# Local and global attention, then eight experts: the first four units in another order, V of batch 1 in later slots, stores of stage two in the middle of the next group

## The chip, the cores and the metric

The kernel runs on one core of a Trainium2 chip. The core's engines each work through a list of their own: PE (TensorE) does matmuls and transposes into PSUM, DVE (VectorE), ACT (ScalarE) and POOL (GpSimd) do the element work, SP only issues DMAs; ACT and POOL issue some as well. Semaphores order the lists against each other. The metric is the device time of one execution in microseconds, as the median over runs; lower is better.

## What is computed

Attention over 8 batches and 8 heads: 512 local positions that see the 32 global keys and a band of 32 positions to each side, and 32 global positions that see everything. Its output, as 4352 rows of 512, goes through a mixture of 8 experts whose weights per row come from a softmax that is normalised over rows and columns eight times.

```python
k_all = np.concatenate([k_g, k_l], axis=2); v_all = np.concatenate([v_g, v_l], axis=2)
out_g = np.matmul(sm(scale * np.matmul(q_g, k_all.transpose(0, 1, 3, 2))), v_all)
s_ll = np.where(np.abs(pos[:, None] - pos[None, :]) <= 32,
                scale * np.matmul(q_l, k_l.transpose(0, 1, 3, 2)), -1e9)
s_lg = scale * np.matmul(q_l, k_g.transpose(0, 1, 3, 2))
out_l = np.matmul(sm(np.concatenate([s_lg, s_ll], axis=-1)), v_all)
x = np.concatenate([out_g, out_l], axis=2)      # rows of H*D = 512
P = np.exp(x @ w_gate - max)
for _ in range(8):                               # rows, then columns
    P /= P.sum(1, keepdims=True) + 1e-09
    P /= P.sum(0, keepdims=True) + 1e-09
    P *= N / E
out = sum(P[:, e:e+1] * (np.maximum(x @ w1[e], 0.0) @ w2[e]) for e in range(E))
```

## The kernel before

The order of the instructions is written out by hand (`manual_schedule`): each engine runs its part in the order of the Python code, and waits where data or a buffer is not ready. DMAs of SP, ACT and POOL stand in those engines' lists too.

**Stage one** is attention. A *unit* `n` is a pair of heads of a batch (4 units to a batch, 32 in all). Its steps:

- `st_A(n)`, L260: PE transposes q and k; DVE copies the keys to `kTe`, ACT spreads the queries to `qbd`.
- `st_B(n, part)`, L281, and for batch 0 `st_B0`, L308: scores of eight windows of 128 keys and the 32 global keys, in three parts. In `st_B0` the mask is added by a matmul (L325), DVE takes the extreme of each row (L330) and ACT the exponential with its row sum (L334). Two parts use PSUM buffers of `ps_sc`, the third one of `ps_mm`.
- `st_N`, L337: DVE divides by the row sums (L341, L342) and POOL does the global keys' part into `Pl` (L346).
- `st_D1`, L349, and `st_D2`, L357: PE transposes the weights; DVE copies the first (`pw`, L355), ACT the second (`pg`, L363).
- `st_E`, L365: PE multiplies with V (`vab`, `vgz`), and ACT writes the result to `xT` (L379).

`select_v`, L145, lays V of a batch out in rows, in two forms (`va`, `vb`), by matmuls with a selection matrix; each of its slots `j` is four matmuls of 512 columns (L150) and a copy from PSUM (L152) by DVE or ACT. It reads `vsr`, which POOL casts (`cast_vrow`, L139) from what `load_vrow` has loaded. Batch 0 needs four slots of each form, batch 1 four of the first and one of the second; two DMAs on ACT (L604, L605) make the rest of the second form of batch 1. Later batches are loaded in other ways.

The loop at L538 runs over the first four units (`s` = 0 to 3), without any expert work. The loop at L585 runs over the other slots; from its first slot on, matmuls of experts 0 and 1 (`f1`, `f2`, L457 and L471) fill PE between the steps. PSUM is full: two buffers each in `ps_mm`, `ps_sc` and `ps_tr`, and one, of two banks, in `ps_po`.

SP's list holds, in this stretch and in order: the vz loads of batch 0, q and k of batch 1, first half, eight loads of `k_g` (L190), V of batch 1, q and k of batch 1, second half, eight loads of `q_g`, four loads of `vgz` of batch 1 (L159, which read what POOL's DMA at L155 wrote), and q and k of batch 2 (L118). A DMA that uses a semaphore again waits until the one before it on that semaphore has landed.

**Between the stages** the gate's probabilities are normalised while the rest of experts 0 and 1 runs.

**Stage two** runs over groups `m` (512 rows; the last, `m` = 8, has 256) and experts 2 to 7, one pair to an iteration of the loop at L908. An iteration multiplies the rows with `w1` of the next pair (`l1`, L741) and does seven products for its own (`product`, L769), which at a group's last expert are added to `o` (L791). SP loads `w1` two pairs ahead (`load_w1`, two buffers), the scaling rows `pb` three ahead, and at expert `e == 4` the start values of the next group (`load_y`, two buffers of `o`). After a group's last pair, `store(m)` writes `o` to the output.

Of the kernel before, what the change touches and what calls it, by code (L numbers as in the profile page):

```python
# [10 lines left out]
FP32 = mybir.dt.float32  # L11
# [12 lines left out]
def kernel(  # L24
# [13 lines left out]
    nc = tc.nc  # L38

    B, H, Sl, Dh = q_l.shape  # L40
    Sg = q_g.shape[2]
    D, E = moe_w_gate.shape
# [45 lines left out]
    with tc.tile_pool(name="att_c", bufs=1) as att_c, \  # L88
# [50 lines left out]
        def cast_vrow(b):  # L139
            f = vraw.pop(b)  # L140
            for g in range(2):
                h = slice(4 * g, 4 * g + 4)
                nc.gpsimd.tensor_copy(out=vsr[:, :, h, :], in_=f[:, h].rearrange("p h s d -> p s h d"))

        def select_v(b, t, js, both=True):  # L145
            for j in js:
                c0 = P * j + HB * t
                pv = ps_mm.tile([P, D], FP32, tag="mm", name="pv")
                for so in range(NJ):
                    nc.tensor.matmul(pv, zsel[:, so, c0 : c0 + P], vsr[:, so], start=(so == 0), stop=(so == NJ - 1))  # L150
                cp = nc.vector.tensor_copy if both and j % 2 == 0 else nc.scalar.copy
                cp(out=vab[b % 2][t][:, j], in_=pv.rearrange("p (h d) -> p h d", h=H))  # L152

        def load_vg(b):
# [2 lines left out]
        def load_vz(b):  # L157
            for i in range(4):
                nc.sync.dma_start(out=vgz[b % 2][W * i : W * (i + 1), i], in_=vg16[b])  # L159
# [28 lines left out]
        def load_g(src, f):  # L188
            for b in range(B):
                nc.sync.dma_start(out=f[GP * b : GP * (b + 1)], in_=src[b].rearrange("h (p s) d -> p h (s d)", s=NJ))  # L190
# [23 lines left out]
        def init_vgz(t, eng):  # L214
            eng.memset(t, 0.0)
# [121 lines left out]
        def st_N(n, i0, i1):  # L337
            d = st[n]
            if i0 == 0:
                d["rs"] = att_wk.tile([P, NHB], FP32, tag="rs", name="rs")  # L340
            nc.vector.reciprocal(out=d["rs"][:, i0:i1], in_=d["sm"][:, i0:i1])  # L341
            nc.vector.tensor_tensor(out=d["Pu"][:, i0:i1, 0:KW], in0=d["Pu"][:, i0:i1, 0:KW],  # L342
                                    in1=d["rs"][:, i0:i1].unsqueeze(2).to_broadcast([P, i1 - i0, KW]), op=ALU.mult)
            if i1 == NHB:
                d["Pl"] = att_wk.tile([P, NHB, Sg], FP16, tag="Pl", name="Pl")
                nc.gpsimd.tensor_tensor(out=d["Pl"], in0=d["Pu"][:, :, KW:SW],  # L346
                                        in1=d["rs"].unsqueeze(2).to_broadcast([P, NHB, Sg]), op=ALU.mult)
# [188 lines left out]
        cast_first(0, 1, nc.scalar.copy)  # L536
        cast_first(1, 1, nc.vector.tensor_copy)
        for s in range(HP):  # L538
            if s >= 1:
                st_D1(s - 1)  # L540
                st_D2(s - 1)
            for part in range(3):
                st_B0(s, part)
            if s == 0:
                cast_vrow(0)
                cast_qk(0, 1, gq)
                load_qk(1, 0, (nc.sync, nc.sync))
                load_g(k_g, kgf)
                load_w1e(0)
                nc.vector.memset(qbd[1], 0.0)  # L550
            elif s == 1:
                load_vrow(1)
                load_qk(1, 1, (nc.sync, nc.sync))
                load_g(q_g, qgf)
                load_vg(1)
                init_vgz(vgz[1], nc.gpsimd)
            elif s == 2:
                load_w2e(0)
                nc.gpsimd.dma_start(out=wg_sb, in_=moe_w_gate.rearrange("(dko dki) e -> dki dko e", dki=P))
                cast_qk(1, 0, gq)  # L560
                gk0 = cast_g(kgf, 0)
                load_vz(1)
            for t in (kTe[s + 2],) if s < 3 else kTe[5:7]:
                nc.vector.memset(t[:, 0:W], 0.0)
                nc.vector.memset(t[:, W + Sl :], 0.0)
            st_A(s + 1)
            st_N(s, 0, 6)
            st_N(s, 6, NHB)
            if s == 1:
                select_v(0, 1, range(NJ))  # L570
            if s >= 1:
                st_E(s - 1)
            if s == 0:
                select_v(0, 0, range(NJ))
            if s == 3:
                transpose_g(gk0, 0, kgT)
                for t in qgbd:
                    nc.vector.memset(t, 0.0)
                cast_vrow(1)
                load_w1e(1)  # L580
                nc.vector.memset(mask[:, :, KW:SW], 0.0)
                nc.scalar.mul(mask[:, :, 0:KW], m16, -HUGE * 8.0)
        gat = {s: s - 5 for s in range(5, 9)}
        gat.update({2 * j + 1: j for j in range(4, NU // 2)})
        for s in range(HP, NU + 1):  # L585
            slot = s
            b, hp = divmod(s, HP)
            g1 = s in gat
            g23 = s - 1 in gat
            if g1:  # L590
                gn = divmod(gat[s], 2)
            if g23:
                gp = divmod(gat[s - 1], 2)
            if s == HP:
                st_D1(s - 1)
                st_D2(s - 1)
                select_v(1, 0, range(2), False)
                st_E(s - 1)
                select_v(1, 0, range(2, NJ), False)
                st_B(s, 0)  # L600
                select_v(1, 1, (NJ - 1,), False)
                slot = s + 1
                va, vb = vab[1]
                nc.scalar.dma_start(out=vb[0:HB, 0 : NJ - 1], in_=va[HB:P, 0 : NJ - 1])  # L604
                nc.scalar.dma_start(out=vb[HB:P, 0 : NJ - 1], in_=va[0:HB, 1:NJ])  # L605
                cast_qk(1, 1, gq)
                load_w2e(1)
            else:
                st_D1(s - 1)
                if g23:  # L610
                    st_GN(*gp)
            if g1 and s > HP + 1:
                st_G0(*gn)
            f1("a")
            f1("a")
            if HP < s < NU:
                st_B(s, 0)
            if s > HP:
                st_D2(s - 1)
            if g23:  # L620
                st_G2(*gp)
            if s < NU:
                st_B(s, 1)
            f2("a")
            if s + 1 < NU:
                st_A(s + 1)
            f1("v")
            if s < NU:
                st_B(s, 2)
                st_N(s, 0, 6)  # L630
            if s > HP:
                st_E(s - 1)
            if s == HP + 1:
                for t, (src, g, dst) in gcast:
                    transpose_g(t, g, dst)
                st_G0(*gn)
            if g23:
                st_G3(*gp)
            f2("a")
            if s < NU:  # L640
                st_N(s, 6, NHB)
            if s == HP:
                gcast = [(cast_g(x[0], x[1]), x) for x in ((kgf, 1, kgT), (qgf, 0, qgT), (qgf, 1, qgT))]
            if s > 2 * HP:
                f1("v")
            if s >= 5 and (s - 5) % HP == 0:
                logits(NJ * ((s - 5) // HP), NJ)
            if g1:
                st_G1(*gn)
            if s < NU and b + 1 < B:  # L650
                if hp == 0:
                    load_qk(b + 1, 0, (nc.sync, nc.sync))
                    load_qk(b + 1, 1, (nc.sync, nc.sync))
                elif hp == 1:
                    cast_qk(b + 1, 0, gq)
                    if b >= 2:
                        load_w1d(b)
                elif hp == 2:
                    vq = load_v(b + 1)
                    run(vq[:3])  # L660
                    cast_qk(b + 1, 1, gq)
                else:
                    run(vq[3:])
            if s == NU - 3:
                load_w1d(E - 1)
# [242 lines left out]
    for i, (m, e) in enumerate(egs):  # L908
        load_w1(i + 2)
        load_pb(i + 3)  # L910
        if e == 4:
            load_y(m + 1)
        if i == NEG_ - 1:
            last_pair(i)
            break
        sums(i)
        if e == 2 and i > 0:
            init_o(m)
        scale_x(i + 2)
        if m == 0 and e + 2 < E:  # L920
            prep_w2c(e + 2)
        for fm in range(3):
            l1(i + 1, fm, ps_rot, "r")
        for q, fm in ((3, 3), (4, 4), (5, 5), (2, 6), (1, 7), (6, None), (7, None)):
            if i == 0 and q == 2:
                init_o(m)
            product(i, q)
            if fm is not None:
                l1(i + 1, fm, ps_rot, "r")
        if e == E - 1:  # L930
            store(m)
    ctx1.__exit__(None, None, None)


# [28 lines left out]
```

## Time and profile before

| | |
|---|---|
| median of 3 runs | 1077.34 us (1076.32 to 1077.87) |
| the profiled execution | 1076.56 us |
| its span, first to last instruction | 1074.8 us |
| PE, DVE, ACT, POOL busy in the span | 1037.4, 687.3, 553.7, 137.2 us |
| mean granted PE clock | 0.988 |

Busy us by stretches of the span:

| stretch | PE | DVE | ACT | granted clock | DMA share |
|---|---|---|---|---|---|
| 0 to 10 us (loads, first casts) | 7.20 | 8.72 | 3.90 | 1.00 | 0.87 |
| 330 to 400 (normalising) | 68.40 | 41.71 | 35.45 | 1.00 | 0.94 |
| 1035 to 1075 (last group) | 31.58 | 20.07 | 12.85 | 0.96 | 0.39 |

The profile gives for each instruction its engine, its line in the kernel, its start and its length, and for idle time what ended it. PE's matmuls overlap one another, so the time from one start to the next is what a matmul costs, and the length shown is longer. A DMA that has been issued lands some us later.

### The profile page before, as it was taken

Reading aid. Unit: us, or ns where it says so; the run is one execution under the profiler, and the core shown is the slowest. Engines: PE = TensorE matmul, PEld = TensorE weight load, DVE = VectorE, ACT = ScalarE, POOL = GpSimd, SP = SyncE. Lnnn points to the kernel's source line nnn. Section 1 sums busy time; section 2 is a strip of 40 time slices with the busy share of each in tenths; the row PEclk is TensorE's granted clock in tenths of the full one; section 3 lists DMA queues with packets and bytes.
Section 4 is the critical chain, followed back from the end, with each engine's and each line's share of the span. In section 5 each row is a group of like instructions: output and inputs, shape, how many; then the busy total and the mean of one; then the engine's idle time right before and its main releaser. Section 6 shows DMA issues by size and latency. Waiting matters only on the chain.

```text
span 1074.8 us, 20827 instructions
## 1 busy us (share of the span) xinstructions
PE 1037.4 (97%) x8444; PEld 665.1 (62%) x8444; DVE 687.3 (64%) x1438; ACT 553.7 (52%) x1345; POOL 137.2 (13%) x224
## 2 busy tenths in 40 slices
PE   7778999999999999999999999999999999999987
PEld 3445555555555456666666666666666666666676
DVE  7566776766675757766576576575484484485475
ACT  5768787787876445334343343343343343343332
POOL 7243413413314300000000000000000000000000
PEclk9789999999999999999999999999999999999999
DMA  9837677677745975423524524425334234234242
GB/s 280 159 104 161 100 181 153 145 176 140 167 104 100 237 229 198 176 98 138 182 93 167 188 82 162 177 99 175 138 138 176 100 138 176 101 144 150 102 159 82
DMA packets 95799, 160.57 MB, mean 149 GB/s; under 512 B 32716, under 2 KB 68696, under 8 KB 84696
## 3 DMA queue, kind: packets, MB, share of 16 engines
q1 hardware_dynamic: 45208, 119.98, 32.4%
q0 software_dynamic: 46736, 20.20, 15.3%
q10 hardware_dynamic: 3760, 19.07, 4.5%
q8 instruction: 66, 1.08, 0.4%
q14 instruction: 29, 0.24, 0.1%
HBM read 149.24 MB, written 33.40 MB: 170 GB/s over the span
## 4 chain that ended last, share of the span: by engine, by line
PE 75%; ACT 11%; DVE 5%; DMA 2%; issue 1%; SPq 0%; POOL 0%; ACTq 0%; DVEq 0%
PE ph L749 32%; PE m L785 20%; PE pm L785 8%; PE ph L457 6%; PE py L471 5%; ACT Pu L305 5%; ACT qbd L279 1%; ACT hT L460 1%; ACT Pg L405 1%; ACT yst L474 1%; DVE m L402 1%; DMA pb<-pd 1%; ACT xT L379 1%; DMA w1s<-w1d 1%; PE ptw L353 1%
## 5 line engine op out<-in xcount | busy, mean ns | idle before, releaser
L751 ACT ACTIVATE h<-ph 128x512 f16<-128x512 f32 (+1 forms) x432 | 247.0, 573 | 397.8 <-PE ph L749 393.9
L749 PE MATMUL ph<-xs,w1s 128*128 128x512 f16 (+1 forms) x1728 | 405.1, 367 | 3.9 <-DMA w1s<-w1d 2.5
L749 PEld LDWEIGHTS <-w1s 128*128 128x128 f16 x1728 | 169.0, 98 | 128.3 <-DMA w1s<-w1d 2.8
L791 DVE SCALAR_TENSOR_TENSOR o<-pm,o 128x512 f32<-128x512 f32 (+1 forms) x106 | 70.5, 666 | 242.5 <-PE pm L785 242.2
L785 PEld LDWEIGHTS <-h 128*128 128x128 f16 x1616 | 158.1, 98 | 48.4
L785 PE MATMUL m<-w2c,s 128*128 128x256 f16 x1212 | 158.3, 273 | 0.0
L785 PEld LDWEIGHTS <-s 128*128 128x128 f16 x1212 | 118.6, 98 | 43.8
L457 PE MATMUL ph<-xT,w1e 128*128 128x512 f16 (+1 forms) x576 | 137.7, 374 | 0.7 <-ACT vb L152 0.7
L471 PE MATMUL py<-w2e,hT 128*128 128x512 f16 x544 | 128.4, 379 | 0.0
L685 DVE TENSOR_TENSOR xs<-xT,pb 128x2048 f16<-128x2048 f16 (+2 forms) x57 | 117.1, 2060 | 9.7 <-DMA pb<-pd 9.7
L785 PE MATMUL m<-w2c,h 128*128 128x256 f16 x808 | 105.5, 273 | 0.0
L785 PE MATMUL pm<-w2c,h 128*128 128x256 f16 x808 | 96.9, 273 | 0.0
L685 DVE TENSOR_TENSOR s<-h 128x2048 f16<-128x2048 f16 (+1 forms) x106 | 92.3, 912 | 4.9 <-ACT h L751 4.9
L305 ACT ACTIVATE Pu<-ms,mx 128x160 f16<-128x160 f32 x224 | 93.6, 419 | 2.4 <-DVE mx L302 0.4
L457 PEld LDWEIGHTS <-w1e 128*128 128x128 f16 x576 | 55.0, 101 | 50.3 <-issue 4.8
L471 PEld LDWEIGHTS <-hT 128*128 128x128 f16 x544 | 49.3, 97 | 51.0
L302 DVE CUSTOM_DVE_ANT_0 ms<-sc,mask 128x160 f32<-128x160 f32 x224 | 59.8, 320 | 27.1 <-PE sc L297 26.6
L460 ACT ACTIVATE hT<-ph 128x512 f16<-128x512 f32 (+1 forms) x91 | 48.7, 558 | 36.4 <-PE ph L457 35.6
L685 DVE TENSOR_TENSOR h<-h 128x1024 f16<-128x1024 f16 (+1 forms) x106 | 65.5, 660 | 0.0
L791 DVE SCALAR_TENSOR_TENSOR o<-m,o 128x512 f32<-128x512 f32 (+1 forms) x90 | 52.2, 652 | 0.4
L474 ACT COPY yst<-py 128x512 f32<-128x512 f32 x68 | 39.4, 579 | 21.9 <-PE py L471 20.4
L346 POOL TENSOR_TENSOR Pl<-Pu,rs 128x256 f16<-128x256 f16 x32 | 24.2, 755 | 205.1 <-ACT yst L474 58.1
(153 smaller groups left out, 1014.0 us busy)
## 6 DMA issues: line engine op xcount, KB each, us to landing
w1s<-w1d SPq DMA_DIRECT2D x54, 1024.0 KB
yd<-yst ACTq DMA_DIRECT2D x16, 1024.0 KB
pb<-pd SPq DMA_DIRECT2D x48, 256.0 KB
o<-yd SPq DMA_DIRECT2D x8, 1024.0 KB
y<-yd SPq DMA_DIRECT2D x8, 1024.0 KB
out_dram<-o SPq DMA_DIRECT2D x8, 1024.0 KB
f<-in_q_l_dram SPq DMA_DIRECT2D x15, 512.0 KB
f<-in_k_l_dram SPq DMA_DIRECT2D x15, 512.0 KB
```

The costliest lines, as they stand in the source:

```text
L302: nc.vector.tensor_tensor_reduce(out=ms[:, ii, :], in0=sc[:, SW * ii : SW * (ii + 1)], in1=mask[:, mi, :], scale=-scale, scalar=BIG, op0=A ...
L305: nc.scalar.activation(out=d["Pu"][:, i, :], in_=ms[:, ii, :], func=AF.Exp, scale=-1.0, bias=d["mx"][:, i : i + 1], accum_out=d["sm"][:, i ...
L346: nc.gpsimd.tensor_tensor(out=d["Pl"], in0=d["Pu"][:, :, KW:SW], in1=d["rs"].unsqueeze(2).to_broadcast([P, NHB, Sg]), op=ALU.mult)
L457: nc.tensor.matmul(ph[:, 0:n], wts[e][0][:, dk, P * fm : P * (fm + 1)], xT[:, dk, c0 : c0 + n], start=(dk == 0), stop=(dk == DP - 1))
L460: nc.scalar.activation(out=hT[:, fm, 0:n], in_=ph[:, 0:n], func=AF.Relu)
L471: nc.tensor.matmul(py, hT[:, fk, P * c : P * (c + 1)], wts[e][1][:, fk, :], start=(fk == 0), stop=(fk == FT - 1))
L474: nc.scalar.copy(out=ys[:, c, :], in_=py)
L685: nc.vector.tensor_tensor(out=out, in0=in0, in1=in1, op=op)
L749: nc.tensor.matmul(ph[:, 0:n], w1s[i][:, dk, P * fm : P * (fm + 1)], xss[i][:, dk, 0:n], start=(dk == 0), stop=(dk == DP - 1))
L751: nc.scalar.activation(out=hs[i][:, fm, 0:n], in_=ph[:, 0:n], func=AF.Relu)
L785: nc.tensor.matmul(pm[:, HD * t : HD * (t + 1)], lhs[0][:, k, lhs[1] + P * t : lhs[1] + P * (t + 1)], w[:, q - 1, k, :], start=(k == 0 and ...
L791: nc.vector.scalar_tensor_tensor(out=o, in0=pm[:, 0 : HD * nt].rearrange("p (t d) -> p t d", d=HD), scalar=sg / float(E), in1=o, op0=ALU.m ...
```

## The change

- In the loop over the first four units, the scores of unit `s` (`st_B0`) come ahead of the transposes of unit `s - 1` (`st_D1`, `st_D2`); in slot 4, `st_B(4, 0)` comes ahead of them too.
- V of batch 0 is laid out straight after `st_A(s + 1)` and ahead of `st_N(s)`. In unit 0, slots `j` = 0 and 1 of it use one two-bank PSUM tile of `ps_po` (`pair`) in place of buffers of `ps_mm`.
- V of batch 1: POOL's cast comes at `s` = 2 and not at 3; slots 0 and 1 run at `s` = 3, slots 2 and 3 and the slot of the second form in slot 4. Its copies alternate between DVE and ACT as those of batch 0 do; before, all were ACT's.
- The loads of `vgz` of batch 1 stand ahead of those of `q_g` in SP's list.
- In stage two, `store(m)` moves from the end of the group to iteration `e == 3` of the next group, after that iteration's loads of `w1` and `pb`; the one of group 7 moves to `e == 6` of the last group.

```diff
--- before.py
+++ after.py
@@ -142,13 +142,13 @@
                 h = slice(4 * g, 4 * g + 4)
                 nc.gpsimd.tensor_copy(out=vsr[:, :, h, :], in_=f[:, h].rearrange("p h s d -> p s h d"))
 
-        def select_v(b, t, js, both=True):
+        def select_v(b, t, js, pair=None):
             for j in js:
                 c0 = P * j + HB * t
-                pv = ps_mm.tile([P, D], FP32, tag="mm", name="pv")
+                pv = ps_mm.tile([P, D], FP32, tag="mm", name="pv") if pair is None or j > 1 else pair[:, j, :]
                 for so in range(NJ):
                     nc.tensor.matmul(pv, zsel[:, so, c0 : c0 + P], vsr[:, so], start=(so == 0), stop=(so == NJ - 1))
-                cp = nc.vector.tensor_copy if both and j % 2 == 0 else nc.scalar.copy
+                cp = nc.vector.tensor_copy if j % 2 == 0 else nc.scalar.copy
                 cp(out=vab[b % 2][t][:, j], in_=pv.rearrange("p (h d) -> p h d", h=H))
 
         def load_vg(b):
@@ -536,11 +536,11 @@
         cast_first(0, 1, nc.scalar.copy)
         cast_first(1, 1, nc.vector.tensor_copy)
         for s in range(HP):
+            for part in range(3):
+                st_B0(s, part)
             if s >= 1:
                 st_D1(s - 1)
                 st_D2(s - 1)
-            for part in range(3):
-                st_B0(s, part)
             if s == 0:
                 cast_vrow(0)
                 cast_qk(0, 1, gq)
@@ -551,32 +551,34 @@
             elif s == 1:
                 load_vrow(1)
                 load_qk(1, 1, (nc.sync, nc.sync))
-                load_g(q_g, qgf)
                 load_vg(1)
                 init_vgz(vgz[1], nc.gpsimd)
+                load_vz(1)
+                load_g(q_g, qgf)
             elif s == 2:
                 load_w2e(0)
                 nc.gpsimd.dma_start(out=wg_sb, in_=moe_w_gate.rearrange("(dko dki) e -> dki dko e", dki=P))
                 cast_qk(1, 0, gq)
                 gk0 = cast_g(kgf, 0)
-                load_vz(1)
             for t in (kTe[s + 2],) if s < 3 else kTe[5:7]:
                 nc.vector.memset(t[:, 0:W], 0.0)
                 nc.vector.memset(t[:, W + Sl :], 0.0)
             st_A(s + 1)
+            if s == 0:
+                select_v(0, 0, range(NJ), ps_po.tile([P, 2, D], FP32, tag="po", name="pv2"))
+            elif s == 1:
+                select_v(0, 1, range(NJ))
             st_N(s, 0, 6)
             st_N(s, 6, NHB)
-            if s == 1:
-                select_v(0, 1, range(NJ))
             if s >= 1:
                 st_E(s - 1)
-            if s == 0:
-                select_v(0, 0, range(NJ))
+            if s == 2:
+                cast_vrow(1)
             if s == 3:
                 transpose_g(gk0, 0, kgT)
                 for t in qgbd:
                     nc.vector.memset(t, 0.0)
-                cast_vrow(1)
+                select_v(1, 0, range(2))
                 load_w1e(1)
                 nc.vector.memset(mask[:, :, KW:SW], 0.0)
                 nc.scalar.mul(mask[:, :, 0:KW], m16, -HUGE * 8.0)
@@ -592,13 +594,12 @@
             if g23:
                 gp = divmod(gat[s - 1], 2)
             if s == HP:
+                st_B(s, 0)
                 st_D1(s - 1)
                 st_D2(s - 1)
-                select_v(1, 0, range(2), False)
+                select_v(1, 0, range(2, NJ))
                 st_E(s - 1)
-                select_v(1, 0, range(2, NJ), False)
-                st_B(s, 0)
-                select_v(1, 1, (NJ - 1,), False)
+                select_v(1, 1, (NJ - 1,))
                 slot = s + 1
                 va, vb = vab[1]
                 nc.scalar.dma_start(out=vb[0:HB, 0 : NJ - 1], in_=va[HB:P, 0 : NJ - 1])
@@ -910,6 +911,8 @@
         load_pb(i + 3)
         if e == 4:
             load_y(m + 1)
+        if m > 0 and e == (3 if m < B else 6):
+            store(m - 1)
         if i == NEG_ - 1:
             last_pair(i)
             break
@@ -927,8 +930,6 @@
             product(i, q)
             if fm is not None:
                 l1(i + 1, fm, ps_rot, "r")
-        if e == E - 1:
-            store(m)
     ctx1.__exit__(None, None, None)
```

## The prediction

> **What bounds the kernel now.** I read first the busy time by stretches, to see where TensorE (PE) is short of work. The columns are from:to, length, then busy us of PE, weight loads, VectorE (DVE), ScalarE (ACT), GpSimd (POOL), then granted clock, DMA share, GB/s.
>
> ```profile
> 10.00:55.00 45.00, 31.42 (x369) 20.06 (x367) 26.96 (x74) 31.72 (x110) 18.97 (x21) 0.85 0.98 210
> 55.00:330.00 275.00, 265.04 (x2982) 156.48 (x2983) 191.07 (x711) 215.47 (x683) 91.24 (x160) 0.98 0.65 143
> 400.00:1035.00 635.00, 633.75 (x4302) 420.87 (x4302) 398.76 (x478) 254.26 (x434) 0.00 (x0) 1.00 0.40 143
> ```
>
> Outside the first 55 us PE is 96% to 100% busy, so time can be had only at the front and in single stalls. In the first 55 us no engine is full: the four units are a chain of hand-overs. So I read the timeline there, PE and ACT, with the idle time before a row and what ended it in brackets.
>
> ```profile
> 10.02 0.40 ACT L334 ACTIVATE Pu<-sc,mx 128x160 f16<-128x160 f32 x1 [1.06 <-DVE mx L330]
> 18.54 0.39 ACT L334 ACTIVATE Pu<-sc,mx 128x160 f16<-128x160 f32 x1 [0.81 <-DVE mx L330]
> 28.06 0.39 ACT L334 ACTIVATE Pu<-sc,mx 128x160 f16<-128x160 f32 x1 [0.87 <-DVE mx L330]
> 34.67 0.39 ACT L334 ACTIVATE Pu<-sc,mx 128x160 f16<-128x160 f32 x1 [1.05 <-DVE mx L330]
> ...
> 31.85 1.01 PE L353 MATMUL ptw<-identity,Pu 128*128 128x128 f16 x8 [2.90 <-DVE rs L341]
> ...
> 41.34 3.52 PE L150 MATMUL pv<-vsr,zsel 128*128 128x512 f16 x8 [1.24 <-POOL vsr L143]
> ...
> 47.70 0.33 DVE L302 CUSTOM_DVE_ANT_0 ms<-sc,mask 128x160 f32<-128x160 f32 x1 [7.08 <-PE sc L297]
> ```
>
> The exponentials of units 0 to 3 start at 10.02, 18.54, 28.06 and 34.67. PE waits 2.90 us for the normalised rows before it transposes; V of batch 1 waits for its cast, and DVE then stands 7.08 us. Third, stretches of the clock's own length (the trace's clock record has half clock from 31.03 to 44.68, 54.92 to 58.34, 65.16 to 68.58: 3.41 us or four times that), and the one stall of stage two, in PE's timeline and the issue queue (SPq):
>
> ```profile
> 27.62:31.03 3.41, 1.33 (x46) 1.11 (x43) 2.42 (x8) 2.97 (x17) 0.17 (x1) 1.00 1.21 231
> 31.03:34.44 3.41, 2.59 (x29) 2.46 (x30) 2.39 (x5) 2.14 (x6) 0.75 (x1) 0.50 0.98 170
> ```
>
> ```profile
> 1026.39 0.60 PE L749 MATMUL ph<-xs,w1s 128*128 128x256 f16 x4
> ...
> 1039.02 1.49 PE L749 MATMUL ph<-xs,w1s 128*128 128x256 f16 x12 [2.48 <-DMA w1s<-w1d]
> ...
> 1031.27 0.39 SPq L795 DMA_DIRECT2D out_dram<-o  x1
> 1031.76 0.45 SPq L705 DMA_DIRECT2D w1s<-w1d  x1
> ```
>
> A stretch with PE busy for 1.33 us is followed by half clock, here until 44.7. At the end, the w1 load's buffer is free at 1026.99 (end of the first row), but its issue stands behind the store, which waits for the last update of `o`; PE then waits 2.48 us for it.
>
> **The stores.** They move from the end of a group to the middle of the next. The load above can go out at 1027.0 and not 1031.76, with no 1 MB in front. Before, store and load together took 7.2 us (31.76 to 38.97); at that price it lands by 1034.2, and PE asks at 1036.5. Gain 2.48 us. The seven earlier boundaries (w1 issued 486.50 where its buffer was free at 483.50) show no PE wait, so they give nothing; their cover is the 11.6 us from 486.50 to the use at 498.10. Queued behind a moved store is the load of `o` one iteration (13.0 us) later, which must now wait until the store has landed; store, w1 and pb together moved in about 9 us at 486 to 495, so it doesn't wait. The last store goes behind the last w1 issue (about 1049) and is over before the final rows at 1068.75. Bounds: 0 if the load were late anyway, 2.8 by the weight-load row.
>
> **Units 0 and 1.** Durations: 4 V matmuls 0.87 us apart; V copy DVE 0.68, ACT 0.58; normalisation on DVE 0.19+0.96+0.16+0.43=1.74; three maxima 1.61; eight exponentials 2.97, starting 0.70 after the first maximum; qbd 1.22; pw 0.69; pg 0.37. V of slots 0 to 2 runs from 10.40 without a wait (slot 0 and 1 have a pair buffer); slot 3 waits for the exponentials (13.04) and ends 14.1, before 16.77. DVE: two V copies to 13.9, normalisation to 15.63, and only then the maxima of unit 1, whose scores are there from 14.8 (qbd ends 14.20). So exponentials at 16.35, not 18.54: 2.2 won. Maxima end 17.26, pw 17.95, and the transposes of unit 2, queued behind pw for a buffer, run at 18.0; exponentials end 19.3, pg and qbd 20.9; V of slots start 18.6, 19.45 (behind the exponentials), 20.4 (behind DVE's copy), 21.5 (behind ACT's copy after qbd); its copy ends 23.2, `st_E` 23.4. Scores of unit 2 at 23.45, exponentials 24.85, not 28.06: 3.2.
>
> **Units 2 and 3.** Maxima end 25.75, pw 26.45, transposes 26.5, exponentials 27.8, qbd 29.35, scores of unit 3 at 29.4. The normalisation starts 27.6 with POOL's casts beside it; that row took 1.70 instead of 0.96 beside a POOL cast at 12.64, so it ends 30.05, exponentials at 30.8, not 34.67: 3.9. Then pw 32.4, transposes 33.05, exponentials end 33.75, pg 34.1, qbd 35.25, `st_E` and the key transposes 35.3. V of batch 1 is now cast on POOL at 29.9 to 31.9 (after Pl; its reader, the last V matmul of batch 0, is long done), so slots 0 and 1 run 35.3 to 37.1 with one copy on DVE (37.05) and one on ACT (37.8). DVE's idle 7.08 us is the cover of the copies moved to it; without it each is 0.68. Mask to 38.25, exponentials of unit 4 to 40.0, pg 40.35, `st_E` 41.1, xT 41.75, last V slot 42.05, its copy 42.7, second f1 matmul 42.8. Before: 49.99. Full-clock gain 7.2 us.
>
> **Half clock.** My new PE timeline has two thin places: 25.6 to 29.0 (transposes 0.6, `st_E` 0.75) and 31.5 to 34.9 (the same), each 1.35 us busy in 3.41, like the 1.33 that was followed by half clock. A boundary of the clock's grid falls right for one of them for most phases. Half clock from about 28.5: scores +0.4, pw +1.0, transposes +1.6, two V slots 1.75 instead of 0.87 each; the end is 2.7 later, gain 4.5. Half clock from about 34.5: the V slots alone, +1.5, gain 5.7. I take 4.8, nearer the first, since the grid of before would allow either. Bounds: 7.2 with none; below nothing, see the last rival.
>
> **DMA and queue order.** SP now issues the four vgz loads ahead of the eight q_g loads. They wait for vg of batch 1: issued 15.30, 10.8 us to landing (26.1). So q_g, issued 22.7 to 37.5 before, goes out 27.8 to about 39.5; POOL reads it at 57.1, now about 50: 8 us of cover; any delay beyond costs PE one for one. The q and k loads of batch 2 (56.40 to 58.05) stand, three of four, behind ACT's copies of V halves, which move with the rest; POOL casts them at 66.9. POOL's own queue: Pl of unit 3 stands behind the V casts (31.9) but is due at 35.1. All at nothing. From the second f1 on the order is the same and PE 96% busy, so the shift is carried to the end.
>
> **Sum.** 4.8 + 2.5 = 7.3. Span 1074.8 to 1067.5; that execution's time was 1076.56, the median of the runs 1077.34, so 1077.34 - 7.3 = **1070.0 us**.
>
> **Rivals.**
> No half clock in the front: 1077.34 - 7.2 - 2.5 = 1067.6. For: my longest idle time of PE is 1.6 us, not 2.90. Against: 1.35 us in a stretch. The Trainium skill, "TensorE: Matmul & The Clock Gate", section "HAM oscillation — how this bites in real kernels", asks only for no idle gap over about 3.4 us, and by it this rival would be the forecast. The trace speaks against that as a bound: 2.90 us of idle was enough.
> DVE becomes the bound: V copies and normalisation stand ahead of the next maxima, and if the normalisation takes 0.74 more beside POOL in three units and not in one, with half clock too, 4.8 - 2 x 0.74 - 0.8 for a maximum waiting on a late V copy = 2.5; 1072.3. For: maxima of unit 1 already wait 0.8 us for DVE. Against: POOL is idle in two of these.
> The w1 load is late anyway: 1077.34 - 4.8 = 1072.5. Against: the 4.8 us between free buffer and issue.
> Slower: half clock from unit 1 on. PE has 1.2 us in the stretch 15.5 to 18.9; if half clock sets in there and no later stretch is full enough to end it, the 14.1 us of PE work from 18 to 37 grow by 0.86 (V rows: 3.52 against 1.89 for eight), 12.1 us. All on the chain: -7.2 + 12.1 - 2.5 = +2.4, 1079.7. It decides when the low clock begins before 20 and holds past 37. Against: V matmuls from 18.6 to 22.4 fill a stretch, and such a stretch (41.27 to 44.68) ended it before.
>
> **Chances.** Forecast 0.50, no half clock 0.20, DVE 0.14, w1 load 0.06, slower 0.06, the rest, between 1073 and 1077, 0.04. 0.2% (2.15 us) is what can be told from no change: faster is below 1075.2. The first four cases are faster nearly throughout, 0.90 with 0.03 off for their tails; same 0.07; slower 0.06. The range holds them from the full-clock gain with one half-clock stretch less later on (1.6 less, 1066.0) up to 1075.5, where 1.8 us of all terms is left (the store's alone would be 1074.9).
>
> **What would show it.** Exponentials of units 1 to 3 near 16.4, 24.9 and 31; second f1 near 43 to 45.5; no wait for w1s at the last group; half clock in one or two stretches before 45. Wrong if PE waits for vgz, q_g or V halves in slots 4 and 5, or if the shift at 55 is gone by 330.

## The result, and the profile after

| | before | after |
|---|---|---|
| median of 4 runs each, same chip | 1077.32 us | 1068.14 us (1067.16 to 1070.00) |
| ratio, 95% interval | | 0.9918 [0.9901, 0.9935] |
| the profiled execution | 1076.56 us | 1068.08 us |
| its span | 1074.8 us | 1066.3 us |
| mean granted PE clock | 0.988 | 0.994 |

The change is faster by 9.2 us by the medians and 8.5 by the two profiled executions; 7.3 were forecast. Two terms make it up, as forecast: the front (the stretch up to 55 us), and the one stall in the last group. How the lead builds up is read from the start of the same instruction in both traces:

| start of, us | before | after | lead |
|---|---|---|---|
| exponentials of unit 0 | 10.02 | 10.44 | -0.42 |
| unit 1 | 18.54 | 18.10 | 0.44 |
| unit 2 | 28.06 | 26.45 | 1.61 |
| unit 3 | 34.67 | 32.31 | 2.36 |
| unit 4 | 48.13 | 41.41 | 6.72 |
| second f1 group (four matmuls at L457) | 49.99 | 45.40 | 4.59 |
| exponentials of unit 5 | 59.74 | 53.92 | 5.82 |
| unit 31 | 330.12 | 324.30 | 5.82 |
| 130th last matmul of `l1` | 1035.28 | 1029.41 | 5.87 |
| 100th last | 1044.27 | 1035.74 | 8.53 |
| end of span | 1074.79 | 1066.27 | 8.52 |

The exponentials of units 1 and 3, from ACT's timeline (start and length in us, engine, line, operation, then the idle time before and what ended it):

```profile
18.10 0.39 ACT L334 ACTIVATE Pu<-sc,mx 128x160 f16<-128x160 f32 x1 [1.47 <-DVE mx L330]
...
32.31 0.39 ACT L334 ACTIVATE Pu<-sc,mx 128x160 f16<-128x160 f32 x1 [0.80 <-DVE mx L330]
```

Units 2 and 3 follow the one in front by 8.35 and 5.86 us; the forecast had 8.5 and 5.95. Only unit 1 is far off: 18.10 instead of 16.35. The chain of waits in time order says why (start, length, engine and tile on the chain):

```profile
11.54 0.94 PE pv L150 x4
12.51 0.70 DVE va L152
13.25 1.90 PE pv L150 x8
15.18 0.69 DVE va L152
16.00 0.96 DVE Pu L342
17.07 0.43 DVE Pu L342
17.49 0.58 DVE mx L330
```

Between V's slot 0 and slot 1 stands slot 0's copy. The timeline has the same wait on PE:

```profile
13.25 2.75 PE L150 MATMUL pv<-vsr,zsel 128*128 128x512 f16 x12 [0.78 <-DVE va L152]
```

The prediction let both slots run back to back because they have a buffer each. But they are two halves of one tile, and the second half's matmuls waited for the first half's copy. All of DVE's work behind it is late by that: V's third copy, the normalisation, the maxima.

V of batch 1 no longer waits for its cast, and DVE's 7.08 us of idle time ahead of the scores of unit 4 (L302) are 1.10. In PE's and DVE's timeline:

```profile
37.22 2.69 PE L150 MATMUL pv<-vsr,zsel 128*128 128x512 f16 x8
...
40.58 1.89 PE L150 MATMUL pv<-vsr,zsel 128*128 128x512 f16 x8
...
40.99 0.33 DVE L302 CUSTOM_DVE_ANT_0 ms<-sc,mask 128x160 f32<-128x160 f32 x1 [1.10 <-ACT mask L584]
```

Eight V matmuls take 2.69 us in the first row and 1.89 in the second: the first lie in half clock in part. In the first 100 us the clock record has half clock from 8.1, 35.4, 59.3 and 93.5 us for 3.41 us each; before, it had 13.7 us from 31.0 and three single ones. The pieces of this record are one or several times 3.41 us long; I call that its grid. By stretches of that grid (length, then busy us of PE, weight loads, DVE, ACT, POOL, then granted clock, DMA share, GB/s):

```profile
4.70:8.10 3.40, 1.26 (x11) 0.55 (x10) 3.40 (x6) 1.80 (x3) 2.94 (x5) 1.00 1.11 331
8.10:11.50 3.40, 3.32 (x37) 3.07 (x38) 3.35 (x7) 1.68 (x7) 2.18 (x3) 0.50 1.09 378
...
28.60:32.00 3.40, 1.99 (x56) 1.73 (x57) 3.32 (x6) 2.87 (x10) 3.40 (x4) 1.00 1.15 245
32.00:35.40 3.40, 1.49 (x25) 1.18 (x22) 2.76 (x11) 3.08 (x17) 2.09 (x3) 1.00 1.16 200
35.40:38.80 3.40, 3.06 (x42) 1.91 (x42) 2.33 (x6) 1.90 (x5) 2.29 (x3) 0.51 0.66 110
```

A stretch with PE busy for 1.26 or 1.49 us is followed by half clock, one with 1.99 is not. In the stretch from 32.0 no idle time of PE is above 1.15 us. But busy time alone doesn't decide: in this trace PE is busy for 1.74 us from 49.05 to 52.46, and full clock follows; from 55.9 to 59.3 it is busy for 1.73, and half clock follows. The last section comes back to this.

At the end, in PE's timeline and the issue queue:

```profile
1021.16 0.32 SPq L706 DMA_DIRECT2D w1s<-w1d  x1
...
1030.50 1.47 PE L750 MATMUL ph<-xs,w1s 128*128 128x256 f16 x12
...
1043.29 0.43 SPq L796 DMA_DIRECT2D out_dram<-o  x1
```

The load of `w1` goes out when its buffer is free, and the matmuls that waited 2.48 us for it wait for nothing. Its group on the page shows the same: 3.9 us of idle time, 2.5 of them for the DMA, before; now

```profile
L750 PE MATMUL ph<-xs,w1s 128*128 128x512 f16 (+1 forms) x1728 | 405.4, 367 | 1.4 <-ACT h L752 0.5
```

### The profile page after: what moved, and what is told of

It is laid out like the page before. It is cut to its first block, busy times and chain, and to the rows that moved or that the text cites. A ratio compares the mean times of both kernels' runs of the same rounds, so it can differ in the third digit from the quotient of the medians.

```text
span 1066.3 us, 20822 instructions
## 1 busy us (share of the span) xinstructions
PE 1033.8 (97%) x8444; PEld 663.5 (62%) x8444; DVE 688.7 (65%) x1440; ACT 552.1 (52%) x1343; POOL 138.0 (13%) x224
## 4 chain that ended last, share of the span: by engine, by line
PE 78%; ACT 12%; DVE 7%; issue 1%; DMA 1%; ACTq 0%; POOL 0%; DVEq 0%
PE ph L750 33%; PE m L786 20%; PE pm L786 8%; PE ph L457 6%; PE py L471 6%; ACT Pu L305 5%; ACT qbd L279 1%; ACT hT L460 1%; ACT Pg L405 1%; DVE m L402 1%; ACT yst L474 1%; DMA pb<-pd 1%; DVE Pu L342 1%; ACT xT L379 1%; PE pv L150 1%
## 5 line engine op out<-in xcount | busy, mean ns | idle before, releaser
L457 PE MATMUL ph<-xT,w1e 128*128 128x512 f16 (+1 forms) x576 | 136.4, 371 | 0.0
L457 PEld LDWEIGHTS <-w1e 128*128 128x128 f16 x576 | 54.6, 100 | 48.6 <-issue 2.2
L302 DVE CUSTOM_DVE_ANT_0 ms<-sc,mask 128x160 f32<-128x160 f32 x224 | 59.8, 320 | 20.9 <-PE sc L297 19.3
L346 POOL TENSOR_TENSOR Pl<-Pu,rs 128x256 f16<-128x256 f16 x32 | 24.2, 757 | 199.1 <-ACT yst L474 58.1
```

Of the source, the lines that this page charges most:

```text
L302: nc.vector.tensor_tensor_reduce(out=ms[:, ii, :], in0=sc[:, SW * ii : SW * (ii + 1)], in1=mask[:, mi, :], scale=-scale, scalar=BIG, op0=A ...
L457: nc.tensor.matmul(ph[:, 0:n], wts[e][0][:, dk, P * fm : P * (fm + 1)], xT[:, dk, c0 : c0 + n], start=(dk == 0), stop=(dk == DP - 1))
```

## The experiments

Each ratio is to runs of the kernel before on the same chip. "f1" is the start of the second f1 group in the profiled execution (49.99 before, 45.40 after).

### The two terms by themselves

**e1_stores**, the kernel before with the move of the stores alone:

```diff
+        if m > 0 and e == (3 if m < B else 6):
+            store(m - 1)
...
-        if e == E - 1:
-            store(m)
```

> The kernel before with the stores moved and nothing else. Theory (the store held up the issue of one w1 load at the last group, PE waited 2.48 us for it, and after the change that wait is gone while the shift goes from 5.83 to 8.53): 2.7 us less than before, about 1074.6, and no PE wait for w1s at the last group. Rival (the load is late for another reason, and the shift at the end comes with the front): no change, 1077.3.

1075.57 us against 1078.33, ratio 0.9974 [0.9964, 0.9983]: 2.8 us. The 130th last matmul of `l1` starts at 1036.57 and the 100th last at 1042.90, 6.33 us apart as in the changed kernel (6.33), and not 8.99 as before. No wait for `w1s` is left.

**e2_front**, the changed kernel with the stores back at the group's end (the same diff, the other way round):

> The changed kernel with the stores at the end of the group, as before. Theory (two gains that add): 5.8 us less than before, about 1071.5, and the wait for w1s is back. Rival (the front's shift is absorbed somewhere without the moved stores): under 4 us less.

1071.05 us, ratio 0.9934 [0.9919, 0.9949]: the front alone is worth some 7 us by this run, and 6 by the ratios of the changed kernel and e1. The wait is back, at a new place of the span:

```profile
1026.98 0.39 SPq L796 DMA_DIRECT2D out_dram<-o  x1
...
1027.47 0.45 SPq L706 DMA_DIRECT2D w1s<-w1d  x1
...
1034.67 1.48 PE L750 MATMUL ph<-xs,w1s 128*128 128x256 f16 x12 [2.43 <-DMA w1s<-w1d]
```

Load behind store, 2.43 us of PE's time. 0.9974 times 0.9934 is 0.9908, and the change has 0.9918 [0.9901, 0.9935]: the terms add, as far as these intervals tell.

### What in the front gives the gain

**e3_order**, the kernel before with the stores (as in e1) and the scores ahead of the transposes; all of V stays where it was:

```diff
+            for part in range(3):
+                st_B0(s, part)
             if s >= 1:
                 st_D1(s - 1)
                 st_D2(s - 1)
-            for part in range(3):
-                st_B0(s, part)
...
             if s == HP:
+                st_B(s, 0)
                 st_D1(s - 1)
...
-                st_B(s, 0)
```

> Stores moved, scores ahead of the transposes in the first four units and slot 4; V laid out where and how it was before. Theory (each part takes a share of the front): about 2 us below the stores alone, 1072.6; exponentials of units 1 to 3 earlier by 0.5, 1 and 1 us. Rival (the order does nothing, since DVE and ACT end the waits): as the stores alone, 1074.6.

1072.42 us, ratio 0.9948 [0.9931, 0.9964]. Its exponentials of unit 4 start at 39.89, 8.2 us ahead of before and even 1.5 ahead of the changed kernel, but the second f1 group at 47.56 is only 2.4 ahead. The start of unit 4 is no lead of the whole: its scores now stand ahead of V in PE's list. V of batch 1 still comes late and with all its copies on ACT, and the experts come behind it:

```profile
38.00 2.01 POOL L143 CAST vsr<-vraw 128x1024 f16<-128x1024 f32 x2
...
40.18 3.36 PE L150 MATMUL pv<-vsr,zsel 128*128 128x512 f16 x8
...
44.10 2.76 PE L150 MATMUL pv<-vsr,zsel 128*128 128x512 f16 x12
...
46.70 1.89 PE L457 MATMUL ph<-xT,w1e 128*128 128x512 f16 x8
```

The cast ends at 40.0, the selection starts at 40.18, and the experts' first matmuls follow its end. Half clock from 36.3 to 43.1 lies over this execution too: the first eight V matmuls take 3.36 us, where eight take 1.89 at full clock, so by this estimate some 1.5 us of the lateness is the clock's.

**e4_vplace**, the changed kernel with the old order of scores and transposes (the diff of e3 the other way round):

> Stores moved, V laid out as in the change (ahead of the normalisation, pair buffer, V of batch 1 in slots 3 and 4), but the transposes ahead of the scores as before. Theory: about 3.5 us below the stores alone, 1071.1; unit 4's exponentials 4 us earlier than before, those of units 1 to 3 hardly. Rival (V is the whole of the front): 1068.8.

1069.40 us, ratio 0.9923 [0.9908, 0.9937]. Units 1 to 4 are later than in the changed kernel (19.50, 28.25, 34.55 and 43.29), yet the second f1 group, at 45.16, is not. The total is nearer to the rival (V is the whole of the front) than to the theory. One trace's f1 is a rough measure, though: the three profiled executions with the changed front have it at 45.40 (the changed kernel), 46.97 (e2) and 48.08 (e0, below).

**e5_v1**, the kernel before with the stores and V of batch 1 alone (cast at `s` = 2, slots 0 and 1 at `s` = 3, the rest in slot 4, copies on two engines, `vgz` ahead of `q_g`):

```diff
...
+            if s == 2:
+                cast_vrow(1)
             if s == 3:
...
-                cast_vrow(1)
+                select_v(1, 0, range(2))
...
-                select_v(1, 0, range(2), False)
+                select_v(1, 0, range(2, NJ))
                 st_E(s - 1)
-                select_v(1, 0, range(2, NJ), False)
                 st_B(s, 0)
-                select_v(1, 1, (NJ - 1,), False)
+                select_v(1, 1, (NJ - 1,))
```

> The kernel before with the stores moved and V of batch 1 alone in the new slots (cast in unit 2, slots 0 and 1 in unit 3, copies on DVE and ACT, vgz loads ahead of q_g); V of batch 0 and the order of scores and transposes as before. Theory (V of batch 1 is nearly the whole of the front): the second f1 at 45 to 46, 1069.5 or a ratio of 0.9925 to 0.993. Rival (V of batch 0 ahead of the normalisation brings half): 0.9945 to 0.995.

1069.60 us, ratio 0.9927 [0.9915, 0.9940]. Taken from e1's 0.9974, V of batch 1 is worth 0.0047 (5.1 us), the order alone 0.0026 (2.8 us), and the whole front 0.0056 (6.0 us). The two come to 7.9 us and so seem to overlap, but the intervals do not settle that. With V of batch 1 in place, the order and V of batch 0 add 0.9 us by the ratios, which the intervals do not tell from nothing. Which part of the move of V of batch 1 does it (the cast, the slots, the copies on two engines or the order of the loads) no run separates.

### The clock

**e0_after**, the changed kernel once more, as the measure for the runs beside it:

> The changed kernel once more, as the yardstick for the runs beside it: 0.992 of the kernel before, three or four stretches of half clock before 100 us in each run, and the runs with less half clock the faster ones, about 0.9 us for 3.41 us of it.

1068.90 us, ratio 0.9918 [0.9905, 0.9932]. This execution has 10.2 us of half clock from 7.8 on: exponentials of unit 1 at 20.56, f1 at 48.08. The same kernel in two executions, 2.7 us apart at f1.

**e6_fill**, the changed kernel with 24 unneeded matmuls of 512 columns, multiplying zeros, in PE's gaps of the first units:

```diff
+        def keep(w, n):
+            for i in range(n):
+                nc.tensor.matmul(w, identity, kTe[NK - 1][:, 0:Sl], start=True, stop=True)
...
+        keep(warm, 4)
         for s in range(HP):
...
                 st_D2(s - 1)
+                wf = ps_po.tile([P, Sl], FP32, tag="po", name="wf")
+                keep(wf, 4)
...
+            if s >= 2:
+                keep(wf, 4)
             st_N(s, 0, 6)
```

> The changed kernel with 24 extra matmuls of zeros, 512 columns wide, that nothing reads, put where PE waits in units 0 to 3 (four behind the first transposes of all, four behind each st_D2 of units 1 to 3, four behind the transposes of units 3 and 4). Theory (thinly filled stretches bring the half clock, and it costs about 0.9 us each on the chain): no half clock between 8 and 50, 1 to 2 us below the changed kernel. Rival (half clock in the front is hidden behind ACT and DVE, or needs a whole idle stretch): same or up to 1 us slower by the extra matmuls.

1067.11 us, ratio 0.9905 [0.9891, 0.9918]: 1.8 us below e0 by the medians (the intervals overlap), with more work on PE. In this trace no half clock falls ahead of 49.5, and f1 starts at 43.59. The stretches of this kernel:

```profile
5.10:8.50 3.40, 2.30 (x19) 1.03 (x18) 3.40 (x6) 2.08 (x4) 3.04 (x5) 1.00 1.12 372
8.50:11.90 3.40, 2.78 (x36) 1.95 (x35) 3.34 (x10) 1.92 (x12) 2.58 (x3) 1.00 1.10 367
...
46.10:49.50 3.40, 0.81 (x13) 0.54 (x12) 2.95 (x10) 2.48 (x9) 0.53 (x1) 1.00 1.12 273
49.50:52.90 3.40, 3.40 (x10) 1.29 (x10) 0.69 (x1) 0.60 (x1) 3.20 (x4) 0.50 1.15 246
```

Where the fill is, the stretch is 2.30 us full and keeps its clock; where none is, 0.81 us are followed by half clock, now in a place where PE is the bound: from f1 to the exponentials of unit 5 it takes 10.2 us here, and 8.5 in the changed kernel. In all fourteen profiled executions that distance is 9.5 to 10.2 us where half clock falls into it (seven) and 8.5 to 8.7 where none does (seven).

### The waits that the prediction missed or weighed

**e7_twotiles**, the changed kernel with slot 1 of unit 0's V in a tile of its own:

```diff
-  pv = ... if pair is None or j > 1 else pair[:, j, :]
+  pv = ... if pair is None or j > 1 else pair[j]
...
-  select_v(0, 0, range(NJ), ps_po.tile([P, 2, D], FP32, tag="po", name="pv2"))
+  select_v(0, 0, range(NJ), (ps_po.tile([P, D], FP32, tag="po", name="pv2"), ps_tr.tile([P, D], FP32, tag="tr", name="pv3")))
```

> The changed kernel with V slot 1 of unit 0 in a PSUM tile of its own (ps_tr) in place of the second half of the pair. Theory (slot 1 waits for the copy of slot 0 because both are one tile, and slot 2, the normalisation and unit 1's maxima wait in turn): unit 1's exponentials about 0.9 us earlier, the second f1 and the total 0.5 to 0.9 less. Rival (ACT and PE of units 2 to 4 take it up): unit 1 earlier and no change at the second f1.

1069.00 us, ratio 0.9915 [0.9901, 0.9928]. The wait is gone: all sixteen V matmuls run in one row.

```profile
10.73 4.80 PE L150 MATMUL pv<-vsr,zsel 128*128 128x512 f16 x16
```

But they run at half clock in part (from 9.7; then from 19.9, 30.2 and 37.0), so unit 1 starts at 17.62 and f1 at 46.57. The total shows nothing, and the trace gives no price, since four stretches of half clock lie over it.

**e8_gs**, the changed kernel with POOL's cast of `k_g` behind the normalisation:

```diff
-                gk0 = cast_g(kgf, 0)
...
             st_N(s, 6, NHB)
+            if s == 2:
+                gk0 = cast_g(kgf, 0)
```

> The changed kernel with POOL's cast of the first four heads of k's global block put behind the normalisation in unit 2, where it stood ahead of it. In the changed kernel VectorE's second product of the normalisation of unit 2 took 1.07 us beside that cast, against 0.43 in other units. Theory (a shared port: VectorE waits for POOL's cast): that product takes 0.43 us, the exponentials of unit 3 start about 0.6 us sooner relative to those of unit 2 (5.2 us behind them, where it was 5.86), and the second f1 group comes up to 0.6 us sooner; total 0 to 0.7 us less. Rival (the front is bound by TensorE's matmuls there, not by VectorE): the product gets shorter, but the second f1 group and the total stay (within 0.5 us of the changed kernel, ratio to before 0.991 to 0.993).

1068.63 us, ratio 0.9913 [0.9898, 0.9927]. DVE's second product, in the changed kernel and in this one:

```profile
30.59 1.07 DVE L342 TENSOR_TENSOR Pu<-Pu,rs 128x256 f16<-128x256 f16 x1
```

```profile
30.11 0.42 DVE L342 TENSOR_TENSOR Pu<-Pu,rs 128x256 f16<-128x256 f16 x1
```

The 0.65 us are real. POOL's own cast (29.59 in the changed kernel, 30.96 in this one) took 1.78 us beside the products and 1.03 behind them. But the exponentials of unit 3 follow those of unit 2 by 6.03 us, where it was 5.86. Half clock from 30.6 lies over this execution, so the next kernel, which has the same edit at full clock there, gives the cleaner reading. Its DVE (line numbers there are four higher, so L346 is L342 and L334 is L330):

```profile
28.55 0.43 DVE L346 TENSOR_TENSOR Pu<-Pu,rs 128x256 f16<-128x256 f16 x1
29.47 1.62 DVE L334 TENSOR_REDUCE mx<-sc 128x3 f32<-128x480 f32 x3 [0.50 <-PE sc L332]
```

DVE is done sooner and waits 0.50 us for the scores. The distance is 5.82 us, against 5.85 in e6, which is at full clock without the edit. The product is off the chain there; the scores end the wait, as the rival has it.

**e9_best**, the three edits of e6, e7 and e8 together:

> The changed kernel with three things together: 24 unneeded matmuls of 512 columns in the gaps of units 0 to 3 (as in e6_fill), the two halves of unit 0's selected V in tiles of their own (as in e7_twotiles), and POOL's cast moved (as in e8_gs). Theory that these are separate costs on the chain: no half clock ahead of 49 us, and the gain of e6_fill (1.8 us against the changed kernel) plus 0.5 to 1.5 us: 1065.5 to 1066.8, ratio to before 0.989 to 0.990. Rival (once the clock holds, the chain of transposes, selections and scores on TensorE sets the front, and the other two waits are covered): as e6_fill, 1067.1, ratio 0.9905.

1065.48 us, ratio 0.9883 [0.9870, 0.9896]; its interval ends below that of e0 (0.9905). It also ends below that of e7 (0.9901), which has the two tiles without the fill and the moved cast: since e8 shows no gain from the cast, this speaks for the fill more clearly than e6 alone. With the clock held, the price of the pair's wait can be read. Here and in e6, neither of which has half clock ahead of 47 us:

```profile
10.34 3.86 PE L150 MATMUL pv<-vsr,zsel 128*128 128x512 f16 x16
```

```profile
12.76 2.75 PE L150 MATMUL pv<-vsr,zsel 128*128 128x512 f16 x12 [1.22 <-DVE va L152]
```

Unit 1, which lies ahead of the moved cast, starts at 16.05 and not 17.61, f1 at 41.97 and not 43.59: 1.6 us, carried whole to f1.

**e10_best**, e9 and eight more unneeded matmuls at slot 4:

```diff
                 st_B(s, 2)
+                if s == HP:
+                    keep(ps_po.tile([P, Sl], FP32, tag="po", name="wf"), 8)
```

> e9_best and 8 more unneeded matmuls behind the scores of unit 4, the place in which e6_fill still had half clock (49.5 to 52.9 us). Theory that each 3.4 us of half clock costs about 0.9 us: that stretch is gone, and the time is 0.5 to 0.9 us below e9_best less the 1.7 us of matmuls where they do not lie in a gap: between 0.9 us less and 0.8 us more. Rival (the clock's stretches are not caused by thin places): a stretch stays within 5 us of that place.

1065.07 us, ratio 0.9873 [0.9857, 0.9888]. The half clock of e9 at 47.7 is gone (the first is now at 57.1), and f1 to unit 5 takes 8.53 us, not 10.14. Of these 1.6 us, 0.79 are left at the end of the span: e10's f1 starts 0.57 us later than e9's, but 0.54 of that is there at unit 1, ahead of the eight matmuls. The intervals do not tell e9 and e10 apart. Both are faster than the changed kernel; e10's profiled execution is 2.2 us below that of the changed kernel.

**e11_vfill**, e4 with the fill of e6, to price the order of scores at full clock:

> The changed kernel with the old order within a unit (transposes of the unit in front ahead of the scores), V of batch 1 in slots 3 and 4 and the stores as in the change, and the 24 unneeded matmuls of e6_fill. It differs from e6_fill in the order alone, with the clock held at full in both as far as it goes. Theory that the order of scores is worth something of its own: the second f1 group comes 0.8 us or more behind that of e6_fill (43.6 us), and the total is 0.6 to 1.5 us above it (1067.7 to 1068.6). Rival (V of batch 1 is the whole of the front's gain, the order only moves the same work about): the second f1 group within 0.5 us of 43.6, the total within 0.5 us of 1067.1.

1071.79 us, ratio 0.9938 [0.9925, 0.9950]. Neither theory had this. The median is 2.4 us above that of e4, the same kernel without the fill, but on another chip; by the ratios to before it is 1.6 us, and the intervals overlap. What the fill costs is plainer in the trace: in the old order PE has no gap behind the transposes of unit 1, and the fill stands ahead of scores that were ready. Unit 2 starts at 29.52 (28.25 in e4, 25.98 in e6).

```profile
27.30 1.02 PE L260 MATMUL wf<-kTe,identity 128*128 128x512 f16 x4
28.16 0.22 PE L329 MATMUL sc<-m,bigI 128*128 128x128 f16 x1
```

So this run has the fill on the chain and does not price the order. What the order is worth by itself at full clock stays open. What the run shows is that in the old order the fill brings no gain, where in the new one there is room for it.

## Why the prediction was right

**Stores**: forecast 2.48, measured 2.66 in the trace (8.53 less 5.87) and 2.8 in e1. The mechanism is shown by e1 and e2. Nothing came late behind the moved store: in the changed kernel PE, DVE and ACT wait for no DMA from 400 us on. (The 7.2 us that the prediction calls store and load together run from the load's issue; from the store's, at 1031.27, they are 7.7, by which the load lands at 1034.7, still ahead of 1036.5.)

**Front**: the term that was mis-sized. 4.8 was taken; the profiled executions give 5.8 from unit 5 to the last group, and the ratios 6.0. (The reading that led there, PE 96% to 100% busy outside the first 55 us, holds up to 1035 us; in the last 40 us PE is busy for 31.58, or 79%.) Step by step:

- *Units 0 and 1, "slot 0 and 1 have a pair buffer", without a wait*: failed. The wait of 0.78 us (1.22 at full clock) was there, and with it unit 1 came at 18.10 where 16.35 was forecast. e9, without it and at full clock, has 16.05.
- *Units 2 and 3*: the distances held within 0.15 us. The cast beside the normalisation was there and cost 0.65 us, where 0.74 was foreseen, but on the second product and not the first; and it was covered: unit 3 follows unit 2 by 5.82 us without it (e9) and 5.85 with it (e6). So the 5.95 for unit 3 came out near, but not through this price: without the cast, the scores of unit 3 are there hardly sooner.
- *V of batch 1 with "DVE's idle 7.08 us as cover"*: right, and more than the prediction made of it. It listed this last, behind the order of scores that it worked through unit by unit; by e5 it is 5.1 of the front's 6.0 us. The leads of units 1 to 3 are mostly not what arrives: e5 has them at 18.55, 29.50 and 36.13, no earlier than before, and its f1 at 46.73 is 3.3 ahead.
- *Full-clock gain 7.2, second f1 at 42.8*: e6, without half clock ahead of 49 us, has 43.59, and e8, with one stretch from 30.6, 43.74. That is 0.8 to 0.9 more than forecast; the pair's wait, 1.6 by e9, is more than all of it.
- *Half clock, 1.5 or 2.7*: 45.40 less e6's 43.59 is 1.8 us in the profiled execution, between the two. One stretch, at 35.4, is near the second place foreseen (34.5); the other, at 8.1, lies over the scores of unit 0, where the prediction did not look. With the pair's wait this makes 4.59 at f1 for the 4.8 taken. That this comes so near is in part luck: errors cancel, and with the same front e2 and e0 have f1 at 46.97 and 48.08, only 3.0 and 1.9 ahead of before.
- *"The shift is carried to the end"*: held from unit 5 on, 5.82 to 5.87 up to the last group. But between f1 and unit 5 the lead grew by 1.23 us. Before had half clock at 54.9 to 58.3 there, and after has its next at 59.3, behind unit 5. The prediction's sum counted nothing for half clock behind f1; only its range had one such stretch less, at 1.6 us. With 0.2 less at f1 and 0.2 more from the stores, this is the 1.2 us by which the forecast was short of the profiled executions. By the medians it was short by 1.9; the four runs of the changed kernel lie 2.8 us apart.

**DMA and queue order at nothing**: right. The four `vgz` loads went out from 27.94, the eight `q_g` loads until 40.6, and POOL read `q_g` at 52.48 without a wait for it.

**Rivals.** DVE as the bound: the normalisation was longer beside POOL in one unit and not in three, and e8 and e9 speak against it there, since a shorter product only made DVE wait. (At unit 1 DVE's copies and normalisation are on the chain, as the forecast had them.) The load late anyway: excluded by e1. The slower case: the half clock in this trace's front is two single stretches; e0, with 10.2 us of it from 7.8, comes nearest and still takes 1070.88 us. No half clock in the front: not what the change does in the executions profiled, but e6, with no half clock ahead of 49.5, has 1067.11 us, near the 1067.6 given for it. That is partly luck: e6 still has the pair's wait, for which this rival has nothing. The Trainium skill's rule ("TensorE: Matmul & The Clock Gate", section "HAM oscillation — how this bites in real kernels"), which asks for no idle gap over about 3.4 us, does not agree with this trace: 1.15 us was the longest gap in the stretch ahead of the half clock at 35.4. (Of the 2.90 us that the prediction set against it, from 28.95 to 31.85, only 2.08 lie ahead of the half clock at 31.03.)

## What to carry to other kernels

In a chain of hand-overs, gains of early steps do not add up: look for the last work that everything behind it waits for (here V of batch 1), and for an engine that stands idle ahead of it. Two halves of one tile were one buffer to whoever waited (1.22 us in e6, nothing in e9); if they are to overlap, make two tiles. Where matmuls are sparse, unneeded ones can go into gaps of TensorE, and only there: e6 and e9, with 24 of them in gaps, are faster than the same kernels without by their medians (e9 clear of the intervals of e7), while in e11 the same 24 stand ahead of work that was ready and bring nothing.

## What the runs showed of the hardware

- *Half clock follows a thin stretch, not a long gap; how thin, busy time tells only roughly.* In the first 100 us of the fourteen profiled executions, every full-clock stretch of the grid with PE busy for up to 1.60 us was followed by half clock (among them 1.26 and 1.49 in after, 0.81 in e6), and none with 2.44 or more. Between these both were seen: 1.73 in after, 1.71 in e8 and 2.43 in e5 were followed by it; 1.74 in after, 1.88 in e8 and this one in before were not (full clock holds there until 31.0):

```profile
10.55:13.96 3.41, 1.66 (x8) 0.67 (x7) 3.03 (x7) 3.39 (x16) 2.51 (x3) 1.00 1.11 335
```

- *Columns sort the cases better than busy time.* A matmul of 64 columns is shown 0.22 us long, like one of 128, though such matmuls start 0.03 to 0.06 us apart. As an estimate, put each matmul at 0.217 us for 512 columns, the distance at which the f1 matmuls follow one another. Then all 51 stretches below 1.40 us were followed by half clock, all those above 1.60 (over 250) by full clock, and of the 12 between, at 1.40 to 1.52, seven by half and five by full. No run varied this by itself.
- *Its price is that of the place.* One stretch costs 0.5 us at unit 1 (18.10 in after against 17.61 in e6), and 1.6 us between f1 and unit 5 (10.14 in e9 against 8.53 in e10), where PE is busy for 3.30 of the 3.40 us. The grid's position differs from execution to execution (the changed kernel's first half clock begins at 8.1 in one and at 7.8 in the other), and the time goes with the half clock: in four runs of the changed kernel 1067.16 us went with a clock of 0.997 and 1070.00 with 0.992.
- *DVE and POOL slow each other.* A product of 0.42 us took 1.07 beside a cast of POOL's, and the cast 1.78 instead of 1.03. The unit's first product, begun ahead of that cast, took 1.04 us with the cast beside it (after) and without it (e9).
